# A fourth tile for transposed q and k, a planner that runs twice and holds loads back, and split banks for the last products

## The chip, the cores and the metric

The kernel runs on one core of one Trainium2 chip. The metric is the device time of one execution in microseconds (us), lower being better. Every run told here was in the fast state, so fast runs are compared with fast runs throughout. An execution of the kernel before takes 291.3 to 295.6 us over the 33 runs that were made beside the experiments, so differences of less than about one per cent need several runs, and one trace is only one execution. A span in a trace is 1.8 to 1.9 us shorter than the time of the same execution.

## The reference

An attention recurrence feeds a mixture of experts. Cut to what matters:

```python
# q, k, v, f_logit: (4, 8, 768, 48): batches, heads, tokens, head size
f = 1 / (1 + exp(-f_logit))
for t in range(768):
    state = f[:, :, t, :, None] * state + einsum('bhd,bhe->bhde', k[:, :, t], v[:, :, t])
    y[:, :, t] = einsum('bhd,bhde->bhe', q[:, :, t], state)
x = y.transpose(0, 2, 1, 3).reshape(3072, 384)
p = domain_probs / (domain_probs.sum(-1, keepdims=True) + 1e-9)      # (3072, 4)
out = sum(p[:, e:e+1] * (maximum(x @ w1[e], 0) @ w2[e]) for e in range(4))   # F = 1024
```

## The kernel before

The tokens are cut into 6 chunks of 128. For a chunk and a batch, q and k are multiplied by exponentials of the summed gates (POOL), transposed by a DMA transpose (`tp`: a `qk` tile becomes a `QK` tile), multiplied with each other on TensorE (`at`), and y comes out. y, scaled by the expert's probability, is transposed by another DMA transpose (`xt`: a `yb` tile becomes a part of an `xT` tile), and the experts' first matmuls (`h`) read it. Most of TensorE's time is these expert matmuls. "tp 2.3" below is the transpose of chunk 2, batch 3.

All these steps are declared to a small planner in the kernel's own Python, with an assumed cost each. It simulates the engines and the buffers and fixes the order in which each engine's instructions are emitted:

```python
rooms = {"ps_m": 7, "ps_t": 0, "f": 2, "q": 2, "k": 2, "v": 2, "gp": 2, "e": 2, "qk": 5,
         "vb": 6, "egs": 8, "QK": 3, "AT": 2, "yb": 4, "xT": 3, "h": 3, "s": 6, "o": 9}

def run(self):
    ...                                            # cut
    for e in ("PE", "ACT", "DVE", "POOL", "DMA"):
        while free_at[e] <= now + 1e-9:
            for o in left:                         # by priority
                if e in o.costs and not (o.port and ...):
                    t = self.ready(o, e)
                    if t is not None and t <= now + 1e-9 and self.take(o):   # inputs there, buffers free
                        break
            ...                                    # cut: o is placed at `now`, or the engine waits
```

The loads of q, k, v and f (384 KB each, two batches of a chunk), the transposes and most stores are all issued by SP, one queue, in planned order. So a load that the planner puts ahead of a transpose is ahead of it on the chip.

```python
def dma_tp(c, b):
    nc.sync.dma_start_transpose(out=tl("QK", c, b)..., in_=tl("qk", c, b)...)
def dma_xt(c, b, g):
    nc.sync.dma_start_transpose(out=tl("xT", c, g)...[:, :, b * T:(b + 1) * T], in_=tl("yb", c, b, g)...)
...
op = P.add(f"ld {nm}{c}.{b}", {"DMA": cost or (0.95 if c else 1.1) * n}, ...)   # loads
P.add(f"tp {c}.{b}", {"DMA": 1.4}, ..., lag=2.5)
P.add(f"xt {c}.{b}.{g}", {"DMA": 1.3}, ..., lag=2.4)
```

For chunks 2 to 5 the experts' second matmuls are seven products of block sums (p1 to p7), each with two halves in one PSUM bank. At the very end, p3 is accumulated onto p5 in p5's bank:

```python
def bank(c, g, r):
    return 5 if r == 3 and (c, g) == (C - 1, NG - 1) else r
```

Of the kernel before, what the change touches and what calls it, by code (L numbers as in the profile page):

```python
# [26 lines left out]
class Plan:  # L27
# [31 lines left out]

    def run(self):  # L60
        for o in self.ops:
            for k in o.frees:
                self.left[k] = self.left.get(k, 0) + 1
        for o in self.ops:
            if o.name.split(" ")[-1].startswith("0.") and set(o.costs) & {"ACT", "DVE"}:
                o.lag += 0.1
        left = sorted(self.ops, key=lambda o: o.prio)
        free_at = {e: 0.0 for o in left for e in o.costs}
# [3 lines left out]
        while left:  # L72
            for f in [f for f in freeing if f[0] <= now + 1e-9]:
                freeing.remove(f)
                self.rooms[f[1]].append(f[2])
            for e in ("PE", "ACT", "DVE", "POOL", "DMA"):
                while free_at[e] <= now + 1e-9:
                    for o in left:
                        if e in o.costs and not (o.port and e in ("DVE", "POOL") and port > now + 1e-9):
                            t = self.ready(o, e)  # L80
                            if t is not None and t <= now + 1e-9 and self.take(o):
                                break
                    else:
                        break
                    left.remove(o)
                    if o.name == "h 0.0.0.0":
                        self.rooms["ps_m"].append(7)
                    o.engine, o.start, o.end = e, now, now + o.costs[e]
                    free_at[e] = o.end
                    if o.port and e in ("DVE", "POOL"):  # L90
                        if e == "POOL" and last is not None and last.engine == "DVE":
                            o.behind = last
                        port, last = o.end, o
                    for k in o.frees:
                        self.left[k] -= 1
                        if self.left[k] == 0:
                            held = o.lag if e == "DMA" or o.name.startswith("egs") else 0.0
                            freeing.append((o.end + held + self.LATENCY, k[0], self.slot[k]))
                    done.append(o)
            nexts = [t for t in free_at.values()] + [f[0] for f in freeing] + [port]  # L100
            for o in left:
                for e in o.costs:
                    nexts.append(self.ready(o, e) or 0.0)
            nexts = [t for t in nexts if t > now + 1e-9]
            if left and not nexts:
                raise RuntimeError("no step can run: " + ", ".join(o.name for o in left[:8]))
            if left:
                now = min(nexts)
# [4 lines left out]
def kernel(  # L113
# [33 lines left out]
    ps = ctx.enter_context(tc.tile_pool(name="ps", bufs=1, space=PS))  # L147
    rooms = {"ps_m": 7, "ps_t": 0, "f": 2, "q": 2, "k": 2, "v": 2, "gp": 2, "e": 2, "qk": 5,
             "vb": 6, "egs": 8, "QK": 3, "AT": 2, "yb": 4, "xT": 3, "h": 3, "s": 6, "o": 9}
    S0 = 2  # L150
# [291 lines left out]

    def bank(c, g, r):
        return 5 if r == 3 and (c, g) == (C - 1, NG - 1) else r

    def mm_p(c, g, r, u):
        for n, e in enumerate(range(g * 2, g * 2 + 2)):
# [4 lines left out]
            for fc in range(KH):  # L452
                nc.tensor.matmul(out=tl("pp_", c, g, bank(c, g, r))[:, u], lhsT=a[:, fc, u * T:(u + 1) * T], rhs=w[:, fc],  # L453
                                 start=(n + fc == 0 and bank(c, g, r) == r and (u == 0 or (c, g, r) != (C - 1, NG - 1, 5))), stop=(n == 1 and fc == KH - 1), skip_group_check=True)

# [10 lines left out]
    def add_load(c, nm, b, n, prio, deps=(), cost=None):  # L466
        op = P.add(f"ld {nm}{c}.{b}", {"DMA": cost or (0.95 if c else 1.1) * n}, lambda e: load(c, nm, b, n), prio,
                   deps=deps, takes=[(nm, c, b // 2)], lag=3.5 if c > 1 else 2.0)
        for i in range(n):
            ld[c, nm, b + i] = op  # L470
        return op
# [41 lines left out]
    def attention(c, slot, gran):  # L513
# [51 lines left out]
        for b in range(B):  # L565
# [12 lines left out]
            if c >= S0:  # L578
                xdone[c, b] = {}
                xe = None  # L580
                for g in range(NG):
                    ex_ = []
                    for e in (2 * g, 2 * g + 1):
                        xe = P.add(f"ev_x{e} {c}.{b}", {"ACT": 0.58, "DVE": 0.63}, lambda eng, b=b, e=e: ev_x(c, b, e, eng), s(11) + 0.1 + 0.01 * e,
                                   deps=[y, pdone, xe], takes=[("yb", c, b, g)], frees=[pt_("y")])
                        ex_.append(xe)
                    xdone[c, b][g] = P.add(f"xt {c}.{b}.{g}", {"DMA": 1.3}, on(dma_xt, g), s(13) + 7 * g, deps=ex_, takes=[("xT", c, g)],
                                           frees=[("yb", c, b, g)], lag=2.4)
# [84 lines left out]
    def add_p(c, g, r):  # L673
        es = (2 * g, 2 * g + 1)
        key = ("ps_m", "pp_", c, g, bank(c, g, r))
        end = (c, g) == (C - 1, NG - 1)
        mm = []
        for u in range(2):
            frees = [("h", c, e, 0) if r in (1, 2, 4, 7) else ("s", c, e, {5: 1, 6: 2, 3: 4}[r]) for e in es]
            mm.append(P.add(f"p{r} {c}.{g}.{u}", {"PE": 0.665}, lambda _, u=u: mm_p(c, g, r, u), unit[0] + 0.5 + 0.01 * u,  # L680
                            deps=[s for e in es for s in hsum[c, e][r]] + [wsum[e] for e in es] + (mm or lastp + ([cdone[c]["r5"]] if end and r == 3 else [])), takes=[key], lag=0.2, frees=frees))
        lastp[:] = mm[-1:]
        src = lambda: tl("pp_", c, g, bank(c, g, r))
        p = unit[0] - 1
        o = lambda nm: tl("o", c, nm)
        last = cdone.setdefault(c, {})

        def read(nm, base, us=slice(0, 2)):
            costs = {"ACT": 0.5, "DVE": 0.52} if base is None else {"DVE": 0.58 if us.stop - us.start == 2 else 0.4}
            last[nm] = P.add(f"{nm} {c}.{g}.{r}", costs, lambda eg: add_c(o(nm), o(base) if base else None, src(), eg, us), p,  # L690
                             deps=[mm[us.stop - 1], last.get(nm), last.get(base)], takes=[("o", c, nm)], frees=[key])

        def plus(nm, other):
            costs = {"DVE": 0.72, "POOL": 1.15}
            if end:
                costs.pop("POOL" if end and nm in ("c21", "c12") else "DVE")
            last[nm] = P.add(f"{nm}+{other} {c}", costs, lambda eg: add_c(o(nm), o(nm), o(other), eg), p + 0.5,
                             deps=[last[nm], last[other]], frees=[("o", c, other)], port=True)

        def send(nm, i, j, us=slice(0, 2)):  # L700
            P.add(f"store {c}.{nm}.{us.start}", {"ACT": 0.6} if us.stop - us.start == 1 else {"DMA": 0.6}, lambda eg: store_c(c, i, j, o(nm), us, eg), p - 25, deps=[last[nm]], frees=[("o", c, nm)], lag=1.5)

# [12 lines left out]
        if not (end and r == 3):  # L715
# [3 lines left out]
            else:  # L719
                read(nm, nm)  # L720
            last[f"r{r}"] = last[nm]
        if r == 2:
            plus("c11", "v1" if end else "u1")
            send("c11", 0, 0)
# [23 lines left out]
        elif r == 3:  # L748
            for u in range(2):
                us = slice(u, u + 1)  # L750
                read("c12", "c12", us)
                send("c12", 0, 1, us)
# [73 lines left out]

    done = P.run()
    first = next(o for o in done if o.name.startswith("h 0.")).start
# [46 lines left out]
```

## Time and profile before

| What | Number |
|---|---|
| Time, median of the 4 runs made with the changed kernel | 292.88 us (292.52 to 293.59) |
| Span of the trace | 291.2 us |
| TensorE busy | 281.4 us (97%) |
| TensorE waits over 0.2 us between 20 and 280 us | 1.97 us for QK at 104.84, 0.27 us for xT at 155.44 |
| Half clock in mid-stream | 105.19 to 108.60 us, which loses 1.71 us of work |
| DMA packets, and of them under 512 B | 157,331; 145,756 |

TensorE is the bound, so time can only come from its few idle microseconds, from its slow clock, or from the two ends. The prediction shows the lines that carry this. In a timeline line, the numbers are the start, the time taken and the engine, and a bracket at the end gives the idle time before the instruction and what ended it. In the SP timeline the second number is the time that issuing took.

### The profile page before, as it was taken

Reading aid. Unit: us, or ns where it says so; the run is one execution under the profiler, and the core shown is the slowest. Engines: PE = TensorE matmul, PEld = TensorE weight load, DVE = VectorE, ACT = ScalarE, POOL = GpSimd, SP = SyncE. Lnnn points to the kernel's source line nnn. Section 1 sums busy time; section 2 is a strip of 40 time slices with the busy share of each in tenths; the row PEclk is TensorE's granted clock in tenths of the full one; section 3 lists DMA queues with packets and bytes.
Section 4 is the critical chain, followed back from the end, with each engine's and each line's share of the span. In section 5 each row is a group of like instructions: output and inputs, shape, how many; then the busy total and the mean of one; then the engine's idle time right before and its main releaser. Section 6 shows DMA issues by size and latency. Waiting matters only on the chain.

```text
span 291.2 us, 6467 instructions
## 1 busy us (share of the span) xinstructions
PE 281.4 (97%) x2521; PEld 195.2 (67%) x2548; DVE 193.7 (67%) x357; ACT 181.8 (62%) x344; POOL 104.0 (36%) x164
## 2 busy tenths in 40 slices
PE   7999999999999979999999999999999999999994
PEld 2666555567777747457776767769567777668694
DVE  4687235798755948478887688777657786642663
ACT  5666556657765817887684686674957672663430
POOL 3785301128387404665234055425354001010011
PEclk9999999999999979999999999999999999999998
DMA  7999999998999999899899977966331935010003
GB/s 153 204 172 206 208 192 203 187 197 189 182 179 181 227 132 181 163 223 199 152 186 188 183 185 127 156 114 92 90 92 36 127 63 94 29 54 0 2 4 108
DMA packets 157331, 41.21 MB, mean 142 GB/s; under 512 B 145756, under 2 KB 156508, under 8 KB 157300
## 3 DMA queue, kind: packets, MB, share of 16 engines
q1 hardware_dynamic: 145764, 33.88, 61.8%
q0 software_dynamic: 11248, 6.72, 16.3%
q8 instruction: 20, 0.33, 0.5%
q10 hardware_dynamic: 288, 0.20, 0.2%
q14 instruction: 11, 0.09, 0.1%
HBM read 31.51 MB, written 4.72 MB: 124 GB/s over the span
## 4 chain that ended last, share of the span: by engine, by line
PE 61%; DMA 3%; issue 1%; ACT 0%; DVE 0%; DVEq 0%; SPq 0%
PE ps L392 30%; PE ps L453 25%; PE ps L407 2%; DMA QK<-qk 2%; PE ps L340 1%; PE ps L355 1%; DMA xT<-yb 1%; PE ps L351 1%; PE ps L361 1%; PE ps L277 1%; ACT h L403 0%; DVE o L459 0%; DVEq L870 0%; SPq L329 0%
## 5 line engine op out<-in xcount | busy, mean ns | idle before, releaser
L392 PE MATMUL ps<-xT,w_sb 128*128 128x512 bf16 (+3 forms) x681 | 140.8, 340 | 1.6 <-DMA xT<-yb 0.3
L403 ACT ACTIVATE h<-ps 128x512 bf16<-128x512 f32 (+2 forms) x181 | 97.3, 542 | 64.6 <-PE ps L392 59.6
L392 PEld LDWEIGHTS <-w_sb 128*128 128x128 bf16 x708 | 66.3, 99 | 47.7 <-issue 0.8
L407 PE MATMUL ps<-w_sb,h 128*128 128x384 bf16 x256 | 50.9, 329 | 0.1
L453 PEld LDWEIGHTS <-h 128*128 128x128 bf16 x512 | 42.6, 98 | 5.4
L459 DVE TENSOR_TENSOR o<-o,ps 128x384 f32<-128x384 f32 (+1 forms) x41 | 21.6, 542 | 25.4 <-PE ps L453 22.6
L453 PEld LDWEIGHTS <-s 128*128 128x128 bf16 x384 | 32.2, 98 | 4.2
L407 PEld LDWEIGHTS <-h 128*128 128x128 bf16 x256 | 24.7, 99 | 15.3 <-issue 0.3
L344 DVE TENSOR_TENSOR AT<-ps,mask 128x512 bf16<-128x512 f32 x48 | 30.4, 683 | 6.3 <-PE ps L340 6.1
L401 DVE TENSOR_SCALAR h<-ps 128x256 bf16<-128x256 f32 (+2 forms) x47 | 25.3, 551 | 10.6 <-PE ps L392 9.8
L297 ACT ACTIVATE e<-ps 128x384 f32<-128x384 f32 x48 | 26.9, 669 | 6.6 <-issue 3.3
L459 POOL TENSOR_TENSOR o<-o,o 128x384 f32<-128x384 f32 x7 | 6.9, 997 | 57.6 <-DVE o L459 54.6
L305 POOL TENSOR_TENSOR qk<-q,e 128x384 bf16<-128x384 f32 x18 | 21.5, 1194 | 16.0 <-ACT e L297 11.9
L372 POOL TENSOR_TENSOR Sf<-Sf,egs 112x192 f32<-112x192 f32 x20 | 10.8, 539 | 44.5 <-DVE Sf L368 14.7
L305 POOL TENSOR_TENSOR qk<-k,e 128x384 bf16<-128x384 f32 x20 | 20.8, 1042 | 13.1 <-ACT egs L299 4.7
L414 DVE SCALAR_TENSOR_TENSOR o<-ps,pn,o 128x384 f32<-128x384 f32 x24 | 14.7, 616 | 15.6 <-PE ps L407 15.5
L324 ACT ACTIVATE yb<-ps,pn 128x384 bf16<-128x384 f32 x42 | 22.5, 586 | 3.5 <-PE ps L355 2.1
L453 PE MATMUL ps<-tw,h 128*128 128x192 bf16 x256 | 24.2, 246 | 0.0
L453 PE MATMUL ps<-w_sb,h 128*128 128x192 bf16 x256 | 23.9, 246 | 0.0
L453 PE MATMUL ps<-w_sb,s 128*128 128x192 bf16 x256 | 23.9, 246 | 0.0
L441 DVE TENSOR_TENSOR s<-h 128x1024 bf16<-128x1024 bf16 x16 | 12.1, 754 | 10.3 <-ACT h L403 9.8
L368 DVE TENSOR_TENSOR Sf<-Sf,ps 48x192 f32<-48x192 f32 x40 | 14.0, 349 | 6.0 <-PE ps L361 5.2
(72 smaller groups left out, 289.7 us busy)
## 6 DMA issues: line engine op xcount, KB each, us to landing
out_dram<-o SPq DMA_DIRECT2D x23, 192.0 KB, 2.7
w_sb<-in_moe_w_dram POOLq DMA_DIRECT2D x5, 768.0 KB, 17.3
k<-in_k_dram SPq DMA_DIRECT2D x10, 384.0 KB, 5.5
q<-in_q_dram SPq DMA_DIRECT2D x10, 384.0 KB, 4.9
v<-in_v_dram SPq DMA_DIRECT2D x10, 384.0 KB, 5.4
f<-in_f_logit_dram SPq DMA_DIRECT2D x9, 384.0 KB, 4.3
w_sb<-in_moe_w_dram POOLq DMA_DIRECT2D x6, 384.0 KB, 8.4
f<-in_f_logit_dram SPq DMA_DIRECT2D x6, 192.0 KB, 3.8
```

The costliest lines, as they stand in the source:

```text
L297: nc.scalar.activation(out=o, in_=i, func=AF.Exp, scale=1.0 if j else -1.0)
L305: return engines[eng].tensor_tensor(out=tl("qk", c, b)[:, j, :, 0:D].rearrange("t (i r) d -> t i r d", r=2), in0=tl("qk"[j], c, b // 2)[:, ...
L324: nc.scalar.activation(out=out, in_=in_, func=AF.Copy, scale=pe)
L344: nc.vector.tensor_tensor(out=tl("AT", c, b)[:, r], in0=tl("A", c, b, r), in1=mask01.unsqueeze(1).broadcast_to([T, NP, T]), op=ALU.mult)
L368: nc.vector.tensor_tensor(out=Sf[rows, b], in0=Sf[rows, b], in1=KV[rows, :, r, :], op=ALU.add)
L392: nc.tensor.matmul(out=hp(c, e, fc, n0, n1, nf)[:, f], lhsT=w1_sb[:, e, kk, (fc + f) * 128:(fc + f + 1) * 128], rhs=x_of(c, e)[:, kk, n0:n ...
L401: nc.vector.tensor_relu(out=dst, in_=src)
L403: nc.scalar.activation(out=dst, in_=src, func=AF.Relu)
L407: nc.tensor.matmul(out=tl("op", c, e, nt, part)[:, cols], lhsT=tl("h", c, e, half_of(c, nt * T))[:, fc, nt * T:(nt + 1) * T], rhs=w2_sb[:, ...
L414: nc.vector.scalar_tensor_tensor(out=o, in0=op, scalar=pe, in1=o, op0=ALU.mult, op1=ALU.add)
L453: nc.tensor.matmul(out=tl("pp_", c, g, bank(c, g, r))[:, u], lhsT=a[:, fc, u * T:(u + 1) * T], rhs=w[:, fc], start=(n + fc == 0 and bank(c ...
L459: return engines[eng].tensor_tensor(out=o[:, us], in0=x[:, us], in1=y[:, us], op=ALU.add)
```

## The change

The intent was to take away the one long wait of TensorE for a QK tile with a fourth QK tile (paid for with a `qk` tile: five with four don't fit in SBUF, the build asks for 114.75 KB per partition where 113.16 are left), to let the planner know from a first pass when transposes become ready and hold back loads that would get ahead of them, and to let the first half of the last products be read while TensorE writes the second.

```diff
-    def run(self):
+    def plan(self, passes):
...
+        soon = {}
+        for i in range(passes):
+            self.rooms, self.slot, self.left = {r: list(x) for r, x in rooms.items()}, {}, {}
...
+            done = self.run(soon)
+            soon = {o: self.ready(o, "DMA") for o in done if o.engine == "DMA" and o.name[:2] in ("tp", "xt")}
+        return done
+    def run(self, soon):
...
                     for o in left:
+                        if e == "DMA" and o.name.startswith("ld") and o.name[4:5] > "2" and any(
+                                x.start is None and now < t < now + o.costs[e] - 0.3 for x, t in soon.items()):
+                            continue
...
-  ... "qk": 5, "vb": 6, "egs": 8, "QK": 3, ...
+  ... "qk": 4, "vb": 6, "egs": 8, "QK": 4, ...
...
-    def bank(c, g, r):
-        return 5 if r == 3 and (c, g) == (C - 1, NG - 1) else r
+    def bank(c, g, r, u):
+        if (c, g) == (C - 1, NG - 1) and r in (3, 5):
+            return 8 if u else 5
+        return r
...
-  {"DMA": cost or (0.95 if c else 1.1) * n}     # planned cost of a load
+  {"DMA": cost or (1.05 if c else 1.1) * n}
-  xt ... {"DMA": 1.3}
+  xt ... {"DMA": 1.2}
...
-    done = P.run()
+    done = P.plan(2)
```

The rest, cut here, lets each half's adds and stores follow its own bank, and replaces an SBUF add on POOL near the end by a PSUM add on DVE.

More of the change, by code (lines that the diff above doesn't have):

```diff
@@ L58, in take @@
         return True
-    def run(self):
+    def plan(self, passes):
+        rooms = {r: list(x) for r, x in self.rooms.items() if r != "ps_t"}
+        for o in self.ops:
+            if o.name.split(" ")[-1].startswith("0.") and set(o.costs) & {"ACT", "DVE"}:
+                o.lag += 0.1
+        soon = {}
+        for i in range(passes):
+            self.rooms, self.slot, self.left = {r: list(x) for r, x in rooms.items()}, {}, {}
+            self.rooms["ps_t"] = self.rooms["ps_m"]
+            for o in self.ops:
+                o.end = o.start = o.engine = o.behind = None
+            done = self.run(soon)
+            soon = {o: self.ready(o, "DMA") for o in done if o.engine == "DMA" and o.name[:2] in ("tp", "xt")}
+        return done
+    def run(self, soon):
         for o in self.ops:
@@ L63, in run @@
                 self.left[k] = self.left.get(k, 0) + 1
-        for o in self.ops:
-            if o.name.split(" ")[-1].startswith("0.") and set(o.costs) & {"ACT", "DVE"}:
-                o.lag += 0.1
         left = sorted(self.ops, key=lambda o: o.prio)
@@ L99, in run @@
                     done.append(o)
-            nexts = [t for t in free_at.values()] + [f[0] for f in freeing] + [port]
+            nexts = [t for t in free_at.values()] + [f[0] for f in freeing] + [port] + list(soon.values())
             for o in left:
@@ L147 @@
     ps = ctx.enter_context(tc.tile_pool(name="ps", bufs=1, space=PS))
-    rooms = {"ps_m": 7, "ps_t": 0, "f": 2, "q": 2, "k": 2, "v": 2, "gp": 2, "e": 2, "qk": 5,
-             "vb": 6, "egs": 8, "QK": 3, "AT": 2, "yb": 4, "xT": 3, "h": 3, "s": 6, "o": 9}
+    rooms = {"ps_m": 7, "ps_t": 0, "f": 2, "q": 2, "k": 2, "v": 2, "gp": 2, "e": 2, "qk": 4,
+             "vb": 6, "egs": 8, "QK": 4, "AT": 2, "yb": 4, "xT": 3, "h": 3, "s": 6, "o": 9}
     S0 = 2
@@ L452, in mm_p @@
             for fc in range(KH):
-                nc.tensor.matmul(out=tl("pp_", c, g, bank(c, g, r))[:, u], lhsT=a[:, fc, u * T:(u + 1) * T], rhs=w[:, fc],
-                                 start=(n + fc == 0 and bank(c, g, r) == r and (u == 0 or (c, g, r) != (C - 1, NG - 1, 5))), stop=(n == 1 and fc == KH - 1), skip_group_check=True)
+                nc.tensor.matmul(out=tl("pp_", c, g, bank(c, g, r, u))[:, u], lhsT=a[:, fc, u * T:(u + 1) * T], rhs=w[:, fc],
+                                 start=(n + fc == 0 and (c, g, r) != (C - 1, NG - 1, 3)), stop=(n == 1 and fc == KH - 1), skip_group_check=True)
     def add_c(o, x, y, eng, us=slice(0, 2)):
@@ L466, in add_load @@
     def add_load(c, nm, b, n, prio, deps=(), cost=None):
-        op = P.add(f"ld {nm}{c}.{b}", {"DMA": cost or (0.95 if c else 1.1) * n}, lambda e: load(c, nm, b, n), prio,
+        op = P.add(f"ld {nm}{c}.{b}", {"DMA": cost or (1.05 if c else 1.1) * n}, lambda e: load(c, nm, b, n), prio,
                    deps=deps, takes=[(nm, c, b // 2)], lag=3.5 if c > 1 else 2.0)
@@ L586, in attention @@
                         ex_.append(xe)
-                    xdone[c, b][g] = P.add(f"xt {c}.{b}.{g}", {"DMA": 1.3}, on(dma_xt, g), s(13) + 7 * g, deps=ex_, takes=[("xT", c, g)],
+                    xdone[c, b][g] = P.add(f"xt {c}.{b}.{g}", {"DMA": 1.2}, on(dma_xt, g), s(13) + 7 * g, deps=ex_, takes=[("xT", c, g)],
                                            frees=[("yb", c, b, g)], lag=2.4)
@@ L674, in add_p @@
         es = (2 * g, 2 * g + 1)
-        key = ("ps_m", "pp_", c, g, bank(c, g, r))
         end = (c, g) == (C - 1, NG - 1)
+        key = lambda u: ("ps_m", "pp_", c, g, bank(c, g, r, u))
+        halves = [slice(0, 1), slice(1, 2)] if key(0) != key(1) else [slice(0, 2)]
+        last = cdone.setdefault(c, {})
         mm = []
@@ L680, in add_p, with read @@
             mm.append(P.add(f"p{r} {c}.{g}.{u}", {"PE": 0.665}, lambda _, u=u: mm_p(c, g, r, u), unit[0] + 0.5 + 0.01 * u,
-                            deps=[s for e in es for s in hsum[c, e][r]] + [wsum[e] for e in es] + (mm or lastp + ([cdone[c]["r5"]] if end and r == 3 else [])), takes=[key], lag=0.2, frees=frees))
+                            deps=[s for e in es for s in hsum[c, e][r]] + [wsum[e] for e in es] + (mm or lastp) + ([last["r5", u]] if end and r == 3 else []), takes=[key(u)], lag=0.2, frees=frees))
         lastp[:] = mm[-1:]
-        src = lambda: tl("pp_", c, g, bank(c, g, r))
         p = unit[0] - 1
         o = lambda nm: tl("o", c, nm)
-        last = cdone.setdefault(c, {})
-        def read(nm, base, us=slice(0, 2)):
-            costs = {"ACT": 0.5, "DVE": 0.52} if base is None else {"DVE": 0.58 if us.stop - us.start == 2 else 0.4}
-            last[nm] = P.add(f"{nm} {c}.{g}.{r}", costs, lambda eg: add_c(o(nm), o(base) if base else None, src(), eg, us), p,
-                             deps=[mm[us.stop - 1], last.get(nm), last.get(base)], takes=[("o", c, nm)], frees=[key])
+        def read(nm, base, deps=()):
+            for us in halves:
+                costs = {"ACT": 0.5, "DVE": 0.52} if base is None else {"DVE": 0.58 if us.stop - us.start == 2 else 0.4}
+                op = P.add(f"{nm} {c}.{g}.{r}", costs, lambda eg, us=us: add_c(o(nm), o(base) if base else None, tl("pp_", c, g, bank(c, g, r, us.start)), eg, us), p,
+                           deps=[mm[us.stop - 1], last.get(nm), last.get(base), *deps], takes=[("o", c, nm)], frees=[key(us.start)])
+                last["r%d" % r, us.start] = op
+                if end and r == 3:
+                    last[nm, us.start] = op
+            last[nm] = op
         def plus(nm, other):
@@ L695, in plus @@
             if end:
-                costs.pop("POOL" if end and nm in ("c21", "c12") else "DVE")
+                costs.pop("DVE" if nm == "c22" else "POOL")
             last[nm] = P.add(f"{nm}+{other} {c}", costs, lambda eg: add_c(o(nm), o(nm), o(other), eg), p + 0.5,
@@ L700, in send @@
         def send(nm, i, j, us=slice(0, 2)):
-            P.add(f"store {c}.{nm}.{us.start}", {"ACT": 0.6} if us.stop - us.start == 1 else {"DMA": 0.6}, lambda eg: store_c(c, i, j, o(nm), us, eg), p - 25, deps=[last[nm]], frees=[("o", c, nm)], lag=1.5)
+            P.add(f"store {c}.{nm}.{us.start}", {"ACT": 0.6} if us.stop - us.start == 1 else {"DMA": 0.6}, lambda eg: store_c(c, i, j, o(nm), us, eg), p - 25, deps=[last.get((nm, us.start), last[nm])], frees=[("o", c, nm)], lag=1.5)
         nm = {1: "u1", 2: "c11", 6: "u2", 7: "u3", 4: "c21", 5: "c22", 3: "c12"}[r]
@@ L720, in add_p @@
                 read(nm, nm)
-            last[f"r{r}"] = last[nm]
-        if r == 2:
-            plus("c11", "v1" if end else "u1")
+        if r == 1 and end:
+            read("c11", "c11", hsum[c, es[1]][6])
+        elif r == 2:
+            if not end:
+                plus("c11", "u1")
             send("c11", 0, 0)
@@ L748, in add_p @@
         elif r == 3:
-            for u in range(2):
-                us = slice(u, u + 1)
-                read("c12", "c12", us)
+            read("c12", "c12")
+            for us in halves:
                 send("c12", 0, 1, us)
```

## The prediction

> **What bounds the kernel now.** I read the page's busy table and its slices first, then the chain that ended last, then TensorE's timeline around the one large gap, then the issuing queue (SP), then the last 6 us.
>
> ```profile
> PE 281.4 (97%) x2521; PEld 195.2 (67%) x2548; DVE 193.7 (67%) x357; ACT 181.8 (62%) x344; POOL 104.0 (36%) x164
> ...
> PE   7999999999999979999999999999999999999994
> ...
> PEclk9999999999999979999999999999999999999998
> ```
>
> TensorE is the bound: 281.4 of 291.2 us, so only 9.8 us are idle on it. The slices (7.3 us each) show where: the first, the last, and one in the middle, the 15th (102 to 109 us), in which the granted clock falls too. Elsewhere no scheduling can win anything unless it shortens TensorE's own work.
>
> The chain of waits, and TensorE's timeline:
>
> ```profile
> 98.73 6.07 DMA QK<-qk
> 104.84 0.40 PE ps L340 x8
> 105.24 0.75 PE ps L392 x3
> 105.99 1.28 PE ps L407 x4
> ...
> 152.54 2.77 DMA xT<-yb
> ```
>
> ```profile
> 102.48 0.40 PE L340 MATMUL ps<-QK 48*128 48x128 bf16 x8
> 104.84 0.40 PE L340 MATMUL ps<-QK 48*128 48x128 bf16 x8 [1.97 <-DMA QK<-qk]
> ```
>
> TensorE stood idle for 1.97 us for the DMA transpose of q and k of chunk 2, batch 3; the other wait on the chain, for xT at 155.4, cost 0.27 us of idle time (TensorE's timeline has that number in brackets). After the first gap the same work takes twice as long: three L392 matmuls 0.75 us, where the chain has 0.33 for three elsewhere; four L407 matmuls 1.28 for 0.65. The stretches table gives the reason (columns: stretch, busy time of PE, PEld, DVE, ACT, POOL, granted clock, DMA share, GB/s):
>
> ```profile
> 103.50:104.80 1.30, 0.00 (x0) 0.00 (x0) 0.89 (x2) 0.00 (x0) 0.00 (x0) 1.00 0.75 151
> 105.20:108.60 3.40, 3.40 (x17) 2.10 (x16) 1.29 (x2) 0.78 (x3) 0.00 (x0) 0.50 0.71 141
> 108.60:112.00 3.40, 3.40 (x51) 2.86 (x50) 1.94 (x5) 2.64 (x7) 1.05 (x3) 1.00 0.97 182
> ```
>
> Half clock for 3.4 us loses 1.7 us of work. So this one late transpose costs 1.97 + 1.7 = 3.7 us. Why it was late, from POOL's timeline (the product) and SP's (the issues):
>
> ```profile
> 93.93 1.00 POOL L305 TENSOR_TENSOR qk<-k,e 128x384 bf16<-128x384 f32 x1
> ```
>
> ```profile
> 92.31 2.81 SPq L318 DMA_TRANSPOSE QK<-qk  x1
> 95.21 1.00 SPq L422 DMA_DIRECT2D out_dram<-o  x2
> 96.27 0.44 SPq L240 DMA_DIRECT2D k<-in_k_dram  x1
> 96.76 1.86 SPq L240 DMA_DIRECT2D q<-in_q_dram  x1
> 98.73 2.75 SPq L318 DMA_TRANSPOSE QK<-qk  x1
> ```
>
> Its input was complete at 94.93, but it was issued at 98.73: three QK tiles were held by batches 0, 1 and 2, and the first comes free when TensorE has finished batch 0's y products, about 97.0. The planner filled that time with two loads of 384 KB, and the transpose then landed 6.1 us after its issue, where the DMA table's median for these is 3.8.
>
> **What the Trainium skill says.** "TensorE: Matmul & The Clock Gate", Part 1 (The HAM clock gate): the clock falls to half after an idle window of about 3.4 us and needs such a window of work to return. The trace agrees on the return (3.4 us at half rate) but not on the trigger: 1.97 us idle was enough. "DMA: Bandwidth & Descriptors", Anatomy of one DMA and Queues, rings and completion order: "DMA engines do not wait on semaphores", the issuing sequencer does, and each engine consumes a queue's descriptors in ring order. So a load issued first delays a transpose twice, at issue and in the rings. The trace agrees: issue to landing is 3.4 us for the transpose at 124.74 with two stores just ahead, 5.4 for the one at 134.95 and 6.1 for the one at 98.73, both with two 384 KB loads ahead. "PSUM — Partial Sum Buffer", PSUM bank collisions: an engine may not read a bank that TensorE is writing, whatever the addresses. That matters for the tail.
>
> **The change part by part.** I compared the built order of both kernels on each engine. TensorE gets exactly the same matmuls, in another order; no work leaves the bound. Five qk tiles become four, three QK tiles become four.
>
> (a) The fourth QK tile. Batch 3's transpose no longer waits for batch 0's y. In the changed order it follows batch 2's with only one store between them, and no load stands between this chunk's first transpose and its last; before, three did. I count the matmuls recorded between the transpose and its readers, at measured spacings (three 256-column L392 0.33 us, four L407 0.65, a batch's y 0.38, its kv 0.17). Before: 5 of the first, 3 of the second = 3.6 us, against a landing of 6.1. After: 6 and 2, two y and two kv = 4.4 us, against 3.4 to 3.8 without loads ahead. The wait goes, with some 0.6 us to spare, and so does the slow clock: -3.7 us.
>
> (b) The second planning pass holds loads of chunks 3 and up back when a transpose will be ready within the load's time. For the xT wait at 155.4 the q load that stood between the last xT transposes moves behind them. The matmuls that cover that transpose shrink from 4.1 to 3.6 us, but the unhindered landing is 2.8 (the chain's 2.77), so I expect the 0.27 us to go: -0.3.
>
> (c) New order, new thin places. By the same count the cover of the last transpose of each chunk goes, for QK, 4.6 to 4.2 (chunk 1), 4.2 to 4.2 (chunk 2, first pair), 4.1 to 3.9 and 3.9 to 3.9 (chunk 3), 5.8 to 4.1 (chunk 4, second pair), and for xT 3.4 to 4.1, 3.5 to 3.3, 4.0 to 3.3. Before, the measured slack between landing and use was only 0.4 to 0.8 us at several of these, and zero at chunk 2's first pair. Chunk 1's last transpose now has a k load directly ahead, which the hold does not cover (it starts at chunk 3): about 4.7 us to landing, as the transpose at 92.31 had behind one load, against 4.2. I allow +0.3 us in all.
>
> (d) The tail. The timelines of TensorE, DVE and ACT's queue end so:
>
> ```profile
> 285.85 1.48 PE L453 MATMUL ps<-w_sb,s 128*128 128x192 bf16 x16
> ...
> 287.37 0.62 DVE L459 TENSOR_TENSOR o<-o,ps 128x192 f32<-128x192 f32 x2 [0.77 <-PE ps L453]
> 287.76 0.88 ACTq L462 DMA_DIRECT2D out_dram<-o  x2
> ```
>
> The last product's first half is complete at 286.67 but its add waits for the other half, in the same bank, until 287.37. With two banks the first add runs at about 286.7, right after the add before it (ends 286.60); the second still starts at 287.37 but alone, so it ends 0.27 us earlier (287.99 to 287.72), and ACT, which now issued its two stores back to back from 287.76 to 288.64, has the first behind it and issues the second at about 287.8 instead of 288.23: -0.4. The second store is what SP waits for last (1.8 us to landing), though the c22 store lands at 289.26, so not much more is to be had. Replacing c11+v1 on POOL (1.0 us) by one more PSUM add on DVE (0.55), and splitting the p5 add into two halves (0.35 each for 0.55), puts 0.7 us on DVE, which idles 0.3 to 0.8 us between the last products; they hide.
>
> Sum: -3.7 - 0.3 + 0.3 - 0.4 = -4.1 us, 293.1 to 289.0. The start (2.0 us of idle), the drain and TensorE's stream stay.
>
> **The rivals.** First, another transpose takes over: a late one with 0.5 to 1 us of idle leaves 289.5 to 290; one that reaches some 2 us brings the half clock again, +3.7, and the time is 292.5 to 293. For it: the thin cover in (c) and the single k load ahead of chunk 1's last transpose. Against it: none of the other transposes in the trace made TensorE wait over 0.3 us at the same cover. Second, the loads that are held back arrive late and POOL's products or the gates wait, moving the delay one step up the pipe; or four qk tiles, one less, stall the products of the next chunk. For it: DMA engines 90% or more busy up to slice 22. Against: POOL is busy 36% and DMA falls to 3 tenths after slice 24, and the held loads move by a few us only while they serve a chunk 20 us or more later. That would be +0.5 to 1 us. Third, the gain is greater: all idle time inside the stream goes. Outside the places named the idle time sums to 1.7 us (9.8 less 2.0 in the first 10 us, 3.9 after 278 us, 2.0 and 0.3 at the two waits), all of it in small pieces; a third of that would make 288.4.
>
> **Range and chances.** 2% faster is 287.3, that is 5.9 us; the idle and slow time named is 4.4, so that would need faster matmuls: 3%. Slower by 2% needs about two more clock falls: 1%. The range reaches from all waits gone (288.0) to one new wait of about 1.5 us (290.7).
>
> **What would show it.** Right: no TensorE wait for QK<-qk over 0.3 us, the clock 1.00 from 20 us to the drain, the slices' 7 at the 15th gone, the transpose of (a) landing in under 4 us, TensorE's busy time about 1.7 us less (the slow matmuls), the first half's add starting before the last matmul ends. Wrong: half clock anywhere in mid-stream, or a new releaser (xT, or an engine) of over 0.5 us on TensorE.

## The result, and the profile after

The changed kernel took 289.87 us (288.84 to 290.66, 4 runs) against 292.88 us for the kernel before. The ratio is 0.9892, with a 95% interval of 0.9855 to 0.9929. A ratio is the mean time of one kernel's fast runs over that of the other's of the same rounds, so it is not quite the ratio of the medians quoted. That is about 1% faster, inside the 2% that count as the same, and 0.9 us from the predicted 289.0. Repeats gave 290.33 and 289.75 us (0.9908 and 0.9886).

The page of the kernel after, busy time and two rows of its slices:

```profile
PE 280.2 (97%) x2519; PEld 194.5 (67%) x2548; DVE 192.0 (67%) x358; ACT 182.4 (63%) x341; POOL 106.7 (37%) x166
...
PE   7999999999999999998999999999999999999994
...
PEclk9999999999999999999999999999999999999999
```

The 7 of the 15th slice and the fall of the clock there are gone. A new 8 stands in the 19th slice (130 to 137 us). TensorE's timeline of the kernel after shows what it is:

```profile
131.47 0.40 PE L355 MATMUL ps<-QK 48*128 48x128 bf16 x8
132.72 0.40 PE L355 MATMUL ps<-QK 48*128 48x128 bf16 x8 [0.85 <-DMA QK<-qk]
```

L355 of the kernel after is L340 of the kernel before. TensorE now waits 0.85 us for a QK tile of chunk 3, where it waited 1.97 us for one of chunk 2. SP's timeline of the kernel after shows the old place and the new one, with the xT transposes of chunk 2 between them:

```profile
94.38 1.29 SPq L333 DMA_TRANSPOSE QK<-qk  x1
95.76 0.53 SPq L437 DMA_DIRECT2D out_dram<-o  x1
96.38 1.27 SPq L333 DMA_TRANSPOSE QK<-qk  x1
...
108.56 0.57 SPq L255 DMA_DIRECT2D q<-in_q_dram  x1
109.24 4.62 SPq L344 DMA_TRANSPOSE xT<-yb  x3
113.92 0.57 SPq L255 DMA_DIRECT2D v<-in_v_dram  x1
114.54 1.57 SPq L255 DMA_DIRECT2D f<-in_f_logit_dram  x1
...
123.14 2.45 SPq L255 DMA_DIRECT2D v<-in_v_dram  x1
125.69 1.40 SPq L437 DMA_DIRECT2D out_dram<-o  x1
127.19 4.05 SPq L333 DMA_TRANSPOSE QK<-qk  x3
```

Batch 3's transpose of chunk 2 (96.38) follows batch 2's with only a store between, and landed at 100.12, 3.74 us after its issue; before it took 6.1. Further down, one load (q) stands ahead of the three xT transposes and two (v, f) come after them. In the kernel before, two stood ahead, v at 108.25 and f; its SP timeline there:

```profile
108.87 1.57 SPq L240 DMA_DIRECT2D f<-in_f_logit_dram  x1
111.37 4.38 SPq L329 DMA_TRANSPOSE xT<-yb  x3
```

At the last place of the kernel after, loads and a store still stand ahead of the transposes of chunk 3. The transpose that TensorE then waits for was issued at 128.58 and landed at 132.68.

The tail, from the timelines of ACT's queue and DVE in the kernel after:

```profile
284.76 1.00 ACTq L479 DMA_DIRECT2D out_dram<-o  x2
285.04 0.35 DVE L476 TENSOR_TENSOR o<-o,ps 128x192 f32<-128x192 f32 x1 [0.31 <-PE ps L470]
```

The last matmul ends at 285.00. The first store is now issued before that, so the first half was read while TensorE still wrote the second. In the kernel before the last matmul ended at 287.33 and the first store left at 287.76.

An account of the two traces: the named wait −1.97, its half clock −1.71, the xT wait −0.27, the new QK wait +0.85, a small new wait for DVE at 103.10 +0.16, a start in which the clock rose later (the first group of expert work begins at 20.21 instead of 19.75) +0.46, the tail −0.09. The sum is −2.57 us; the spans differ by 288.76 − 291.19 = −2.43 us. So these two executions look as if the fourth tile had done nearly all of it. The experiments test that.

### The profile page after: what moved, and what is told of

Its sections match the earlier page's. It is cut to its first block, busy times and chain, and to the rows that moved or that the text cites. A ratio compares the mean times of both kernels' runs of the same rounds, so it can differ in the third digit from the quotient of the medians.

```text
span 288.8 us, 6467 instructions
## 1 busy us (share of the span) xinstructions
PE 280.2 (97%) x2519; PEld 194.5 (67%) x2548; DVE 192.0 (67%) x358; ACT 182.4 (63%) x341; POOL 106.7 (37%) x166
## 4 chain that ended last, share of the span: by engine, by line
PE 92%; DMA 4%; issue 1%; DVE 1%; ACT 1%; POOL 0%; SPq 0%; POOLq 0%
PE ps L407 40%; PE ps L470 25%; PE ps L422 15%; PE ps L861 3%; PE ps L355 2%; PE ps L370 2%; DMA q<-in_q_dram 2%; DMA QK<-qk 1%; PE ps L292 1%; PE ps L366 1%; PE ps L376 1%; PE ps L329 1%; DMA f<-in_f_logit_dram 1%; PE ps L395 0%; POOL qk L320 0%
## 5 line engine op out<-in xcount | busy, mean ns | idle before, releaser
L418 ACT ACTIVATE h<-ps 128x512 bf16<-128x512 f32 (+2 forms) x178 | 96.1, 545 | 57.1 <-PE ps L407 51.7
L407 PEld LDWEIGHTS <-w_sb 128*128 128x128 bf16 x708 | 65.4, 98 | 45.7 <-issue 0.4
L422 PE MATMUL ps<-w_sb,h 128*128 128x384 bf16 x256 | 50.0, 327 | 0.2 <-DVE Sf L383 0.2
L416 DVE TENSOR_SCALAR h<-ps 128x256 bf16<-128x256 f32 (+2 forms) x50 | 26.1, 537 | 13.8 <-PE ps L407 13.1
L476 POOL TENSOR_TENSOR o<-o,o 128x384 f32<-128x384 f32 x8 | 8.0, 994 | 66.0 <-DVE o L476 65.5
L341 DVE TENSOR_SCALAR yb<-ps,pn 128x384 bf16<-128x384 f32 x23 | 13.5, 613 | 4.6 <-PE ps L370 2.8
```

Source lines behind the costliest of these rows:

```text
L341: nc.vector.tensor_single_scalar(out=out, in_=in_, scalar=pe, op=ALU.mult)
L407: nc.tensor.matmul(out=hp(c, e, fc, n0, n1, nf)[:, f], lhsT=w1_sb[:, e, kk, (fc + f) * 128:(fc + f + 1) * 128], rhs=x_of(c, e)[:, kk, n0:n ...
L416: nc.vector.tensor_relu(out=dst, in_=src)
L418: nc.scalar.activation(out=dst, in_=src, func=AF.Relu)
L422: nc.tensor.matmul(out=tl("op", c, e, nt, part)[:, cols], lhsT=tl("h", c, e, half_of(c, nt * T))[:, fc, nt * T:(nt + 1) * T], rhs=w2_sb[:, ...
L476: return engines[eng].tensor_tensor(out=o[:, us], in0=x[:, us], in1=y[:, us], op=ALU.add)
```

## The experiments

Three theories were on trial. The tile theory says that the fourth QK tile is the gain, as the prediction had it. The order theory says that the gain is in when loads stand ahead of transposes, so that the second pass carries it, and that the tile alone would only move the wait. The clock theory says that what matters is that TensorE's wait made the clock fall. The runs went in three sets, each on another chip: the first four rows of the table, then from `after_again` to `pass3`, then the last four. Each set shared its runs of the kernel before, with medians of 292.96, 292.85 and 293.15 us (11 runs each), so medians are compared within a set and ratios across sets.

| Run | Median us (lowest to highest, runs) | Ratio to before [95%] |
|---|---|---|
| `tile`: only the rooms | 294.48 (293.75–296.09, 6) | 1.0069 [1.0043, 1.0094] |
| `tail`: only the split banks | 293.30 (291.37–294.61, 6) | 1.0016 [0.9979, 1.0053] |
| `fill`: before, with dummy work in the wait | 291.90 (291.48–293.57, 6) | 0.9983 [0.9959, 1.0007] |
| `pass1`: changed, one pass | 293.77 (292.95–293.97, 4) | 1.0032 [1.0009, 1.0055] |
| `after_again` | 290.33 (290.22–291.56, 6) | 0.9908 [0.9858, 0.9959] |
| `notile`: changed, old rooms | 290.60 (290.20–292.25, 4) | 0.9919 [0.9860, 0.9978] |
| `nocost`: changed, old planned costs | 289.76 (288.34–290.60, 6) | 0.9875 [0.9826, 0.9923] |
| `pass3`: changed, three passes | 289.56 (288.39–290.81, 6) | 0.9873 [0.9824, 0.9923] |
| `tile_fat`: tile, loads in long rows | 289.75 (289.07–290.37, 4) | 0.9875 [0.9830, 0.9920] |
| `plan`: only the second pass | 291.27 (289.88–291.88, 4) | 0.9915 [0.9860, 0.9970] |
| `cand`: an attempt to beat both | 289.52 (288.69–291.31, 6) | 0.9878 [0.9834, 0.9921] |
| `after_third` | 289.75 (289.63–290.96, 6) | 0.9886 [0.9849, 0.9924] |

### The fourth tile alone (`tile`)

```diff
-  "qk": 5, ... "QK": 3
+  "qk": 4, ... "QK": 4
```

TensorE's order is the same as before's (in the traces all 2548 weight loads come in the same order, by tile and shape); SP's differs in one place, tp 2.3, which goes ahead of the loads of k and q.

> The kernel before with four QK tiles and four qk tiles, nothing else. The built order differs from before in one place: the transpose of chunk 2, batch 3 stands before the two loads instead of behind them, with 7.3 us of matmuls between it and its readers instead of 3.6; TensorE's order is the same. Theory (the tile makes the gain): no wait for QK<-qk near 105 us, no half clock there, 3.4 to 3.7 us less than before (ratio near 0.988); the xT wait of 0.27 us at about 152 us stays. Rival (the second planning pass, or the whole re-ordering, makes the gain): within 1 us of before.

It was slower than the kernel before: 294.48 us. In its trace tp 2.3 was issued at 95.41, the wait at 105 us is gone and the clock stays full there. But TensorE's timeline has five waits, 4.47 us together (the last is the old one of 0.27 us, grown to 0.82):

```profile
115.52 2.75 PE L392 MATMUL ps<-xT,w_sb 128*128 128x512 bf16 x11 [1.86 <-DMA xT<-yb]
...
128.87 0.40 PE L340 MATMUL ps<-QK 48*128 48x128 bf16 x8 [0.39 <-DMA QK<-qk]
...
130.16 0.40 PE L340 MATMUL ps<-QK 48*128 48x128 bf16 x8 [0.90 <-DMA QK<-qk]
...
141.10 0.40 PE L340 MATMUL ps<-QK 48*128 48x128 bf16 x8 [0.50 <-DMA QK<-qk]
...
156.12 2.75 PE L392 MATMUL ps<-xT,w_sb 128*128 128x512 bf16 x11 [0.82 <-DMA xT<-yb]
```

SP's timeline of the same run gives the cause of the first:

```profile
107.29 0.57 SPq L240 DMA_DIRECT2D v<-in_v_dram  x1
107.91 1.51 SPq L240 DMA_DIRECT2D f<-in_f_logit_dram  x1
109.53 5.53 SPq L329 DMA_TRANSPOSE xT<-yb  x3
```

In the kernel before, TensorE reached this group of L392 at 117.57 without a wait. Here, without its stop at 105, it was there at 115.52 − 1.86 = 113.66, 3.9 us sooner. The three transposes went out only 111.37 − 109.53 = 1.84 us sooner, behind the same two loads, and the one that TensorE waited for, the second of them by the chain of waits, landed at 115.27. The old wait had been hiding this transpose. The spans agree: before had 1.97 + 1.71 + 0.27 = 3.95 us of waits and slow clock, this one 4.47, and the spans are 291.19 and 291.84. The profiled execution was the fastest of the six; what made the others slower still was not traced. The tile theory falls for the tile alone.

### The split banks alone (`tail`)

```diff
-    def bank(c, g, r):  ...                      # with mm_p, read, plus and send as before
+    def bank(c, g, r, u):  ...                   # and their changed versions; rooms, costs and run() as before
```

> The kernel before with the last products' halves in two PSUM banks, c11+v1 as a PSUM add, and nothing else. The pair of profiles puts the gain at 0.1 us from the last matmul to the end (the second store is issued 0.5 us earlier but lands 0.4 us later); my prediction was 0.4. Expected: 0.1 to 0.4 us less than before, ratio 0.9985 to 1.000, hardly to be told from it. Rival (the bank split holds more, by freeing TensorE from a wait in the last products): 1 us or more.

293.30 us, a ratio whose interval holds 1. The trace settles what the times can't: from the last matmul's end to the last instruction it is 3.82 to 3.86 us in the traces with the old tail (`tile`, `fill`, `plan`, `tile_fat` and before) and 3.74 to 3.77 us in those with the new one (`tail`, the three of the changed kernel, `pass1`, `notile`, `nocost`, `pass3`, `cand`). So the new tail gains some 0.08 us.

This trace tells something else too. Up to the last products the order is that of before, but the clock did not fall, and the waits were spread otherwise: 1.58 us for QK at 105.45, 0.34 and 0.79 us for xT at 117.02 and 155.52. Its span, 291.18 us, is that of before all the same.

### Dummy work in the wait (`fill`)

```diff
     def pe_at(c, b):
         QK = tl("QK", c, b)
+        for _ in range(8 if (c, b) == (2, 3) else 0):
+            nc.tensor.matmul(out=<the A tile, before it is written>, lhsT=busy, rhs=<512 columns of busy>, start=True, stop=True)
```

> The kernel before, the late transpose left as it is, but eight dummy matmuls of 512 columns (8 x 0.216 = 1.7 us) put into the 1.97 us in which TensorE waits for it, written to the bank that the next matmuls overwrite. Theory (the idle time itself makes the clock fall, and that costs 1.7 us of the 3.7): the wait stays as work, the clock stays at 1.00 to the end, 1.5 to 1.7 us less than before (ratio near 0.994). Rival (the clock falls for another cause, or costs nothing on the path): the same time as before, or 0.2 more.

TensorE's timeline, and the stretches table (its columns are as in the prediction), of this run:

```profile
103.01 1.90 PE L338 MATMUL ps<-busy 128*128 128x512 bf16 x8
104.94 0.40 PE L342 MATMUL ps<-QK 48*128 48x128 bf16 x8
```

```profile
105.20:108.60 3.40, 3.40 (x45) 2.82 (x40) 1.50 (x3) 2.15 (x6) 0.00 (x0) 1.00 0.72 137
```

The dummies fill the wait, the transpose is as late as before, and the clock in the stretch that ran at 0.50 before is now 1.00. The time fell by 1.06 us in the medians, with an interval that reaches just above 1, and less than the 1.5 to 1.7 us that the clock theory needs. The records of the kernel before suggest why: of its 33 runs beside these experiments only 7 have a mean granted clock of 0.994 or less, as a half-clock stretch makes it, and these are not slower than the others (means of 292.7, 292.6 and 293.0 us in the three sets, against 292.8, 293.35 and 293.5). The half clock of the profiled execution is real but not typical.

### The changed kernel with one pass (`pass1`)

```diff
-    done = P.plan(2)
+    done = P.plan(1)
```

In the first pass nothing is known of coming transposes, so no load is held. The fourth tile, the new planned costs and the new tail stay.

> The changed kernel with one planning pass, so that no load is held back; tiles, planned costs and tail as changed. In its order only 0.7 us of matmuls lie between the xT transpose of chunk 2, batch 3 and its first reader (4.1 us in the changed kernel), against 2.8 us to landing. Theory (the second pass repairs what the new planned costs would do there): a wait of 2 to 3 us for xT near 117 us, perhaps the half clock behind it, 2 to 4 us more than the changed kernel, so 292 to 294. Rival (the second pass is worth nothing): 289 to 290.

293.77 us: nothing of the gain is left. TensorE's timeline and the stretches of this run:

```profile
117.19 3.18 PE L407 MATMUL ps<-xT,w_sb 128*128 128x512 bf16 x9 [2.53 <-DMA xT<-yb]
```

```profile
118.50:121.90 3.40, 3.40 (x10) 1.16 (x9) 0.00 (x0) 1.93 (x4) 1.35 (x2) 0.50 1.09 215
```

It is the xT transpose of chunk 2 again, later still, and this time with a half-clock stretch of its own. The gain hangs on the second pass.

### The changed kernel without the fourth tile (`notile`), and the second pass alone (`plan`)

```diff
 notile                                   plan (from the kernel before)
-  "qk": 4, ... "QK": 4                   +  plan(), run(soon) and the hold
+  "qk": 5, ... "QK": 3                   -    done = P.run()
                                          +    done = P.plan(2)
```

> The changed kernel with three QK tiles and five qk tiles as before; second pass, costs and tail as changed. Theory now (the tile and the hold are worth something only together: the tile lets a transpose go early, the hold keeps the loads from taking its place): chunk 2, batch 3's transpose again waits for batch 0's y and has two loads ahead, cover 4.8 us against about 6 to landing, and the last xT transposes of chunk 2 have only 1.3 us of cover; waits of 1 us and 1.5 us, so 292 to 294. Rival (the second pass alone makes the gain): within 0.7 us of the changed kernel.

> The kernel before with the second planning pass and its hold alone: three QK tiles, five qk tiles, old planned costs, old tail. The changed kernel without the fourth tile had nearly the whole gain (ratio 0.992 beside 0.991). Theory (the hold carries it): ratio 0.990 to 0.995, 290 to 291.5, no wait of over 0.5 us for QK near 105 us. Rival (the hold needs the new costs or the tail): within 0.2% of before.

`notile` took 290.60 us, 0.3 more than the changed kernel of the same set (290.33), where the tile theory expected most of the gain to be lost. `plan` took 291.27 us, a ratio of 0.9915, with three QK tiles, the old costs and the old tail. The loads of chunk 3 that the pass holds back are those that stand among the transposes of chunk 2. SP's and TensorE's timelines of `plan`:

```profile
95.45 0.44 SPq L255 DMA_DIRECT2D f<-in_f_logit_dram  x1
95.94 1.50 SPq L255 DMA_DIRECT2D k<-in_k_dram  x1
98.06 1.86 SPq L333 DMA_TRANSPOSE QK<-qk  x1
```

```profile
117.37 2.98 PE L407 MATMUL ps<-xT,w_sb 128*128 128x512 bf16 x13 [1.51 <-DMA xT<-yb]
```

The q load that stood between k's and tp 2.3 has moved behind it, tp 2.3 landed 4.0 us after its issue (102.09) and TensorE did not wait for it, although there are still only three QK tiles. Two loads are still just ahead of it, f and k where it was k and q, but they went out 0.8 us sooner than those two. So the named wait can be had away without a fourth tile. In this trace the xT wait of chunk 2 remains. In `notile` a wait of 1.68 us stands before the corresponding group at 118.23. The trace names no releaser for it, but an xT transpose (issued at 114.70) landed just before, at 118.14.

One rival stays open. The second pass doesn't only move loads: `plan`'s weight loads leave the order of the kernel before from 102.5 us on, and those of the changed kernel differ from `pass1`'s too, so TensorE's matmuls are reordered. No run held the loads back and kept TensorE's order. That the pass carries the gain is shown; how much of it comes from the loads' places and how much from the new order of the matmuls is not.

### The changed kernel with old planned costs (`nocost`) and with three passes (`pass3`)

```diff
 nocost                                          pass3
-  (1.05 if c else 1.1) * n      # loads         -    done = P.plan(2)
+  (0.95 if c else 1.1) * n                      +    done = P.plan(3)
-  xt {"DMA": 1.2}
+  xt {"DMA": 1.3}
```

> The changed kernel with the planned costs of before (a load 0.95 us a batch instead of 1.05, an xT transpose 1.3 instead of 1.2); tiles, second pass and tail as changed. In its order no cover is thinner than in the changed kernel but for chunk 3's first pair (3.9 us in both), and chunk 2's last xT transpose has 4.4 us. Theory (tile and second pass carry the gain, the costs only decide which order comes out): within 1 us of the changed kernel, either way, 289 to 290.5. Rival (the new costs are what made the order good): 291.5 or more.

> The changed kernel with a third planning pass. Its order has no thinner cover than the changed one's (chunk 3's second pair 4.4 us with loads farther ahead instead of 3.9, the others equal but for chunk 4's first pair, 4.7 instead of 6.7). Expected: the changed kernel's time less up to 0.5 us; above it by 1 us or more would say that cover counted in matmuls does not foretell the waits.

289.76 and 289.56 us, so neither the new costs nor a third pass matter beyond what the runs resolve: the intervals of both overlap that of the changed kernel. The trace of `nocost` has one wait over 0.3 us, 0.49 us for a weight at 20.86, and none after it. This is the whole change without its cost terms, and it has no QK wait at chunk 3.

### The fourth tile alone with loads in long rows (`tile_fat`)

This kernel computes a wrong result on purpose (relative error 0.845). It is `tile`, but the loads of chunks 3 to 5 read the same number of bytes from wrong places in memory, as rows of 3 KB instead of rows of 192 bytes.

```diff
+        src = srcs[nm][c, :, b * H:(b + n) * H, :]
+        if c >= 3:
+            x = (2 * c + b // 2) * 2 * HD
+            src = <the whole tensor, flat, as 128 rows>[:, x:x + 2 * HD]
```

> Wrong result on purpose. The kernel with the fourth tile alone, order unchanged, but the loads of chunks 3 to 5 take the same number of bytes from another place, in rows of 3 KB instead of 192 bytes, so that they hold the DMA engines for less time. Theory (the waits that came up with the fourth tile, for xT at 116 us and QK at 129, 130 and 141 us, are there because loads lie ahead of the transposes in the queue): those waits go or fall under 0.3 us each, 3 to 4.5 us less than with the tile alone, so 290 to 291.5. Rival (the producers on POOL, ACT or DVE are late, the loads only lie beside): the waits stay, 293.5 or more.

289.75 us, against 294.48 for `tile`. The page of this run:

```profile
PE   7999999999999999999999999999999999999994
...
DMA packets 111251, 41.21 MB, mean 143 GB/s; under 512 B 96604, under 2 KB 107356, under 8 KB 111220
```

The bytes are the same and 29% of the packets are gone. The slices have no dent left, and TensorE's timeline has no wait over 0.3 us after 17.7 us. Issue order and buffers are those of `tile`. So the waits of `tile` come from the time that loads of short rows take, and for the first of them, at 115.52, that is time in the queue ahead of transposes, as the order theory says: the v and f loads there landed 3.6 and 4.0 us after their issue instead of 4.2 and 5.6. For the waits for QK the run doesn't separate this from q and k arriving sooner at POOL. (A gentler version, with loads split over partitions, was rejected before it ran, for a read of memory not yet written; no run of it is on record.)

### An attempt to beat both (`cand`), and the repeats

```diff
-  o.name[4:5] > "2"          # hold loads of chunks 3 and up
+  o.name[4:5] > "1"
-  load cost 1.05, tp lag 2.5, xt lag 2.4
+  load cost 0.95, tp lag 2.8, xt lag 2.8
```

> An attempt to beat both: the changed kernel with the planner told what the traces show (2.8 us instead of 2.5 from the end of a QK transpose's issue, 2.8 instead of 2.4 for xT), the loads' planned cost of before, and chunk 2's loads held back too. Its covers are 3.9 to 7.9 us, the thinnest of chunk 3 are 4.6 and 5.7 where the changed kernel has 3.9. Expected: no wait for a transpose over 0.3 us, 1 us less than the changed kernel, 289 to 289.5; no better than it would say that what is left is at the start and in the weights' loads.

> The changed kernel itself, as the mark for the other runs of this job and for a second trace. Expected: ratio to before near 0.989 again. If the 0.85 us wait for QK<-qk near 132 us belongs to its order (cover 3.9 us against 4.1 us to landing), it stands in this trace too, between 0.3 and 1.2 us; if it was a chance of that execution, it is gone.

> The changed kernel as the mark for the attempt, on the same chip: 289.5 to 290.5, and again the wait of 0.8 to 1.2 us for QK<-qk near 132 us.

`cand` plans with landing times nearer to the measured medians of its transposes (3.0 us for xT, 3.7 for QK in the trace after) and holds loads of chunk 2 as well. After 17.1 us its trace has only two waits, of 0.11 and 0.10 us, and its span is 287.3 us. But its time, 289.52 us against 289.75 for the changed kernel in the same set, is not a resolved gain, so no version here is shown to beat the changed kernel. The repeats' traces have the chunk 3 wait again, at 1.15 us (132.40) and 0.41 us (131.87), the second less than the 0.8 us expected.

## Why the prediction was right or wrong

**The total** was right: 289.0 predicted, 289.87 measured, in the range, and within 2% as it was given 96 in 100. It was right partly by luck, because two of its terms were wrong in opposite directions.

**(a) The fourth tile, −3.7 us.** What it said of the place itself held: the transpose landed in 3.74 us, the wait went, the clock stayed. The step that failed is "The wait goes, with some 0.6 us to spare, and so does the slow clock: -3.7 us", as an account of what the tile is worth. The tile alone made the kernel 0.7% slower. The argument checked the cover of the later transposes in the changed order (step c), but as a matter of how many matmuls lie between a transpose and its reader; it did not ask how much sooner TensorE would come by when the first stop was gone. The answer was 3.9 us sooner, for transposes that went out 1.84 us sooner behind the same loads. This is its first rival, "another transpose takes over", which holds for the tile without the second pass. Moreover, 1.71 of the 3.7 us were a half-clock stretch that 26 of 33 runs of the kernel before, by their mean clock, don't show, so the profiled execution's loss was taken for the usual one. `tail`, with before's order, shows an execution that has no half clock, other waits, and the same span.

**(b) The second pass, −0.3 us.** The mechanism was right (loads go behind transposes, the xT wait at 155.4 is gone), and this is the term that was mis-sized. Alone it measured 291.27 − 293.15 = −1.9 us; with all but the fourth tile 290.60 − 292.85 = −2.3 us; and taking it out of the changed kernel left +0.8 us against before (293.77 − 292.96). It was sized by the one wait that the trace of before showed. With the fourth tile its work is at the xT transposes of chunk 2 near 115 us, which made nobody wait in that trace because TensorE was already late. There two loads ahead of three transposes became one, and the 2.53 us that `pass1` waits there are gone. Without the fourth tile, in `plan`, it took away the wait for QK near 105 us and left 1.51 us for xT at 117.37. What the fourth tile adds once the pass is there is not resolved: 0.3 us in the medians of one set.

**(c) New thin places, +0.3 us.** The wait came at a place that was named: the first pair of chunk 3, whose cover shrank from 4.1 to 3.9 us. Three traces have 0.85, 1.15 and 0.41 us there, 0.8 in the mean. The landing took 4.1 us (128.58 to 132.68) with loads and a store ahead. The place feared most, chunk 1's last transpose with a k load directly ahead, did not bite: it had 3.08 us to spare.

**(d) The tail, −0.4 us.** The reading of the banks was right (the page cited has an exception for other groups of 32 partitions, which doesn't arise here, as both halves fill all 128), and the first half's add and store start before the last matmul ends. Relative to that end, the two stores go out at −0.24 and +0.42 us instead of +0.42 and +0.90. But the end moved by 0.08 us only. The prediction saw that the c22 store bounds the gain and took 0.4 all the same. In the trace after that store lands 2.25 us after the last matmul instead of 1.92, and SP's last wait for a store ends at +2.55 instead of +2.65. Why it lands later was not tested; that it shares the DMA engines with a half that now leaves sooner is a guess.

**The rivals.** The second, that held loads arrive late or that four qk tiles starve POOL, left no trace on TensorE: no wait of it for another engine in mid-stream is over 0.2 us. The third, that small idle pieces go too, doesn't show either; what the start lost (0.46 us) is of the size of the differences between executions. In arguing the second, the prediction read the slices loosely: four of DMA's first 22 (1, 10, 17 and 20) are under 90%, and they fall to 3 tenths only at slice 29.

**Its markers.** "No TensorE wait for QK<-qk over 0.3 us" failed, the clock at 1.00 to the drain held, the landing under 4 us held, and TensorE's busy time fell by 281.42 − 280.17 = 1.25 us, less than the 1.7 expected, which the slower start may explain in part. The full clock at 105 us and the missing wait there hold in `tile` too, which was slower; only taking the change apart told.

**What stays open.** Whether the pass gains by the places of the loads or by the new order of the matmuls; how what the changed kernel has over the pass alone (1.5 us in the medians of `plan`'s set, where the intervals overlap) divides among the tile, the costs and the tail; and what the unprofiled executions of before lose where, since only one of them was traced.

## What to carry to other kernels

Before you take away a wait, ask what will come next on the waiting engine, and whether that is made sooner by as much as the engine arrives sooner: a wait can shield a later one. Where loads and transposes share one queue in order, what stands ahead in the queue can be worth more than another buffer, and shorter time in the queue (longer rows) more than either. Size a term from several executions: a clock fall that a trace shows in full may be missing from most runs.

## What the Trainium skill lacked or had wrong

- "TensorE: Matmul & The Clock Gate", Part 1, has the clock fall after an idle window of some 3.4 us and gives no share of a window that is enough; for short idle times it tells only of a case in which many of them made the clock swing. Here it fell although TensorE idled for only a part of such a window: 1.97 us of the 3.41 us before the fall (58%) in the trace of before, and 2.10 us (62%) in `pass1`. It did not fall with 1.68 us (49%, `notile`), 1.58 us (46%, `tail`) and 1.54 us (45%, `tile`). But at the end of the kernel after, one window (283.56 to 286.97 us) is idle from 285.00 on, 1.97 us again, and the clock did not fall until the next one had passed, at 290.38 us. So the idle share alone, as these traces show it, gives no sharp limit. The page's free-running window of 3413 ns and its half rate agree: the rises and falls lie 28 windows (9.615 to 105.188 us) apart in before, and the slow stretches last 3.41 us.
- "DMA: Bandwidth & Descriptors", Latency and other measured facts, has a bandwidth for DMA transposes, 261 GB/s, and no time from issue to landing for small ones between tiles in SBUF ("VectorE: DVE Perf Modes" has 1309 ns for one of 128x128). An estimate from the bandwidth for 128x1024 bf16 (256 KB) would be 1.0 us; with the fixed cost of some 2 us per DMA that the page fits for another issuing path, 3.0 us. Here a QK transpose took 3.0 us with an empty queue, as that sum has it, and 6.1 us with two loads of 384 KB ahead; an xT transpose (128x768) took 2.7 us at best.
- The same page's Specifications ask for at least 512 B per transfer for full rate. The runs agree in direction (3.6 and 4.0 us to landing for two loads in rows of 3 KB, 4.2 and 5.6 us in rows of 192 B) and show what it is worth to others in the queue: with 3 KB rows for the loads of three chunks, 4.47 us of TensorE's waits for transposes went.
